# Weights start 64 bytes, no longer 192, past a multiple of 256 bytes in SBUF: attention over channels and a squared-ReLU FFN on one core

## The chip, the cores and the metric

The kernel runs on one core of a Trainium2 chip. The metric is the device time of one execution in microseconds (us); the time of a version is the median of its runs.

## What is computed

```
B, N, C = 4, 6080, 256;  d_ff = 2048
qn = q / (norm(q, axis=N) + 1e-6);  kn = k / (norm(k, axis=N) + 1e-6)
a  = softmax(kn^T @ qn / tau, last axis) (+ 1e-9)      # 256 x 256 for each of the 4 batches
x  = v @ a                                             # 24320 tokens x 256
h  = relu(x @ w_in)                                    # 256 -> 2048
out = (h * h) @ w_out                                  # 2048 -> 256
```

q, k, v and the output are float32; w_in and w_out arrive as float64, and the kernel makes a high and a low part of each.

## The kernel before

Attention and the first FFN product are folded into one: for each batch the kernel makes W = a @ w_in and then computes relu(v @ W). Tokens stand along the free axis and channels on the partitions. A number is held as a high and a low part (float32r), and each product is three products: high x high, high x low, low x high. Of the 12 token blocks of a batch ten have 512 tokens and the last two 480; after the first two blocks of the program each product of a 2x2 block form is made with seven block products, so that a matmul streams half a block, 256 or 240 columns.

In every matmul of TensorE one operand is fixed (the weights, 128 columns of 4 bytes, 512 bytes in each partition) and one moves (256 or 240 columns, up to 1,024 bytes in a partition). For each matmul the weights are loaded anew; the loading of the next matmul's weights runs while this one streams.

The work is written out as a repeating period (`PERIOD`, `period(k)`), a group of 42 matmuls of the first product and 42 (in six early groups 45) of the second each:

- `first_B`, `second_B` write ps_b, `first_H`, `second_H` ps_h, `copy_C`, `second_C`, `third_C`, `fourth_C` ps_c: six matmuls each, weights from the tiles wf (reloaded for each group from HBM by `load_forms`), moving operands v_hi and v_lo;
- `window_A1` to `window_A3` and `window_S` write ps_o: weights from W_out's own parts (wo_hi, wo_lo) or from sums of them (wS_hi, wS_lo, wS_odd_hi, wS_odd_lo), moving operands A_hi, A_lo, s_hi, s_lo;
- beside them stand the gram of the next batch's q and k (`products`, weights and moving operand both in qk_parts) and the forming of W (ps_w: weights eT_hi, eT_lo).

Where a tile begins in a partition follows from the order of the pools and the sizes ahead of it. In bytes, modulo 256, before the change:

| operands | tiles | start modulo 256 |
|---|---|---|
| fixed | wo_hi, wo_lo (pool const) | 192 |
| fixed | wf, w_hi, w_lo (wpool); wS, wS_odd, eT (wsums); the k half of qk_parts (the first tile of pool) | 192 |
| moving | v_hi, v_lo, A, s1, s2, g parts, the q half of qk_parts | 0 |

The two halves of qk_parts are `HALF` elements (4,096 bytes) apart and `GAP` elements more, which sets the second half, and all tiles of pool behind it, to 0. The seven blocks of v_hi and v_lo follow each other (`T1, B11, T3, B21, B22, T2, T4 = range(7)`). A block of 256 columns is 1,024 bytes, so that all seven begin at 0; a block of 240 columns is 960 bytes, so that blocks 0 to 6 begin at 0, 192, 128, 64, 0, 192, 128.

Of the kernel before, what the change touches and what calls it, by code (L numbers as in the profile page):

```python
# [10 lines left out]
F32 = mybir.dt.float32  # L11
# [21 lines left out]
def kernel(  # L33
# [26 lines left out]
    P = 128  # L60
# [38 lines left out]
    const = ctx.enter_context(tc.tile_pool(name="const", bufs=1))  # L99
# [24 lines left out]
    rinv_room = const.tile([P, NC], F32, name="rinv_room")  # L124

    HALF = NC * GRP
    GAP = 16

    def parts_room(name, dt):

        return pool.tile([P, 2 * HALF + GAP], dt, tag="qk_parts", name=name, bufs=1)

    scalar.activation(parts_room("first", F32)[:, 0:1], exp_bias, AF.Square)
    wo_hi = const.tile([P, NF, C], F32R, name="wo_hi")
    wo_lo = const.tile([P, NF, C], F32R, name="wo_lo")
    late = {}

    def two_parts(name, dt, shape):

        room = parts_room(name, dt)  # L140
        halves = room[:, 0:HALF], room[:, HALF + GAP :]
        return [half.rearrange("p (a b) -> p a b", a=shape[1]) if len(shape) > 2 else half for half in halves]

    def rounded_qk(name):
# [3 lines left out]
        for at in (0, J * C):  # L148
            of_k = room[:, at : at + J * C]
            both = bass.AP(of_k.tensor, of_k.offset, [of_k.ap[0], [HALF + GAP, 2], of_k.ap[1]])  # L150
            parts.append(both.rearrange("p a (j c) -> p a j c", j=J))
# [1435 lines left out]
```

## Time and profile before

| | |
|---|---|
| median of 3 runs | 2107.0 us (2104.4 to 2107.66) |
| the profiled execution | 2107.39 us, its span 2105.6 us, 1.8 us around it |
| TensorE (PE), share of the span | 2100.4 us, 100%, 17,158 matmul records |
| VectorE (DVE), ScalarE (ACT), GpSimd (POOL) | 90%, 89%, 17% |
| granted TensorE clock | 1.00 |
| DMA | 261 GB/s on average |

A busy PE is not a PE at its peak: the end of a matmul is modelled and lies behind the start of the next one. What a matmul costs on PE is read from one start to the next. 17,158 is more than the 17,011 matmuls of the program, since a float32 product stands as two records.

### The profile page before, as it was taken

Reading aid. Unit: us, or ns where it says so; the run is one execution under the profiler, and the core shown is the slowest. Engines: PE = TensorE matmul, PEld = TensorE weight load, DVE = VectorE, ACT = ScalarE, POOL = GpSimd, SP = SyncE. Lnnn points to the kernel's source line nnn. Section 1 sums busy time; section 2 is a strip of 40 time slices with the busy share of each in tenths; the row PEclk is TensorE's granted clock in tenths of the full one; section 3 lists DMA queues with packets and bytes.
Section 4 is the critical chain, followed back from the end, with each engine's and each line's share of the span. In section 5 each row is a group of like instructions: output and inputs, shape, how many; then the busy total and the mean of one; then the engine's idle time right before and its main releaser. Section 6 shows DMA issues by size and latency. Waiting matters only on the chain.

```text
span 2105.6 us, 43463 instructions
## 1 busy us (share of the span) xinstructions
PE 2100.4 (100%) x17158; PEld 2065.7 (98%) x17158; DVE 1905.2 (90%) x2195; ACT 1879.6 (89%) x2379; POOL 350.2 (17%) x430
## 2 busy tenths in 40 slices
PE   9999999999999999999999999999999999999999
PEld 8789999999999999999999999999999999999999
DVE  7898999989999999989998999998999888888887
ACT  5888999889999999889989999998988988988987
POOL 0000111111121111111122111211111121121112
PEclk9999999999999999999999999999999999999999
DMA  9777888789999888788999978878999787787775
GB/s 357 224 230 274 247 267 250 243 253 309 307 278 317 257 247 255 237 253 281 292 299 277 308 251 260 247 243 248 287 278 304 233 239 246 235 242 243 232 242 154
DMA packets 258012, 549.78 MB, mean 261 GB/s; under 512 B 26672, under 2 KB 113072, under 8 KB 257808
## 3 DMA queue, kind: packets, MB, share of 16 engines
q1 hardware_dynamic: 201456, 469.02, 65.0%
q0 software_dynamic: 56352, 77.98, 18.6%
q8 instruction: 135, 2.21, 0.4%
q14 instruction: 69, 0.57, 0.1%
HBM read 433.59 MB, written 58.72 MB: 234 GB/s over the span
## 4 chain that ended last, share of the span: by engine, by line
PE 99%; ACT 0%; DVE 0%; issue 0%; DVEq 0%; ACTq 0%
PE ps_o L29 45%; PE ps_c L29 18%; PE ps_h L29 14%; PE ps_b L29 12%; PE gram L29 7%; PE ps_w L29 2%; PE ps_end L29 0%; PE ps_first L29 0%; PE ps_n L29 0%; ACT x L29 0%; PE ps_t L29 0%; DVE x L29 0%; DVE w_lo L29 0%; ACT A_hi L29 0%; ACT ps_c L29 0%
## 5 line engine op out<-in xcount | busy, mean ns | idle before, releaser
L29 PE MATMUL ps_c<-v_hi,wf 128*128 128x256 f32 (+1 forms) x2208 | 477.1, 279 | 0.3 <-DVE x L29 0.2
L29 DVE TENSOR_TENSOR x<-x 128x1024 f32<-128x1024 f32 (+2 forms) x549 | 464.9, 847 | 11.1
L29 POOL DMA_DIRECT2D o<-o x225 | 232.6, 1188 | 1401.6 <-ACT o L29 903.4
L29 DVE TENSOR_TENSOR s_lo<-x,s_hi 128x1024 fp32r<-128x1024 f32 (+1 forms) x366 | 441.2, 1207 | 16.6 <-ACT s_hi L29 16.2
L29 ACT ACTIVATE x<-x 128x1536 f32<-128x1536 f32 (+4 forms) x384 | 405.2, 1055 | 42.5 <-DVE x L29 38.9
L29 ACT CAST s_hi<-x 128x1024 fp32r<-128x1024 f32 (+1 forms) x366 | 382.3, 1044 | 50.1 <-DVE x L29 49.1
L29 DVE TENSOR_TENSOR A_lo<-x,A_hi 128x1536 fp32r<-128x1536 f32 (+2 forms) x183 | 313.5, 1713 | 83.1 <-ACT A_hi L29 75.0
L29 PEld LDWEIGHTS ps_c<-v_hi,wf 128*128 128x128 f32 x2208 | 375.4, 188 | 1.1 <-DVE x L29 0.4
L29 PE MATMUL ps_b<-v_hi,wf 128*128 128x256 f32 (+1 forms) x1472 | 317.3, 278 | 0.0
L29 PE MATMUL ps_h<-v_hi,wf 128*128 128x256 f32 (+1 forms) x1472 | 317.3, 278 | 0.0
L29 PE MATMUL ps_c<-v_lo,wf 128*128 128x256 f32 (+1 forms) x1104 | 307.5, 279 | 0.0
L29 ACT CAST A_hi<-x 128x1536 fp32r<-128x1536 f32 (+2 forms) x183 | 264.1, 1443 | 0.0
L29 PEld LDWEIGHTS ps_h<-v_hi,wf 128*128 128x128 f32 x1472 | 250.4, 188 | 0.0
L29 PEld LDWEIGHTS ps_b<-v_hi,wf 128*128 128x128 f32 x1472 | 250.3, 188 | 0.1
L29 PEld LDWEIGHTS ps_c<-v_lo,wf 128*128 128x128 f32 x1104 | 207.5, 188 | 0.1
L29 PE MATMUL ps_h<-v_lo,wf 128*128 128x256 f32 (+1 forms) x736 | 204.9, 278 | 0.0
L29 PE MATMUL ps_b<-v_lo,wf 128*128 128x256 f32 (+1 forms) x736 | 204.8, 278 | 0.0
L29 PE MATMUL ps_o<-A_hi,wo_hi 128*128 128x256 f32 (+1 forms) x897 | 193.3, 279 | 0.0
L29 PE MATMUL ps_o<-A_lo,wo_hi 128*128 128x256 f32 (+1 forms) x897 | 193.0, 279 | 0.0
L29 PE MATMUL ps_o<-A_hi,wo_lo 128*128 128x256 f32 (+1 forms) x897 | 192.6, 279 | 0.0
L29 ACT COPY x<-ps_c 128x512 f32<-128x512 f32 (+1 forms) x184 | 107.2, 582 | 53.1 <-PE ps_c L29 42.7
L29 PE MATMUL ps_o<-s_hi,wS_hi 128*128 128x256 f32 (+1 forms) x549 | 153.0, 279 | 0.0
(172 smaller groups left out, 5197.6 us busy)
## 6 DMA issues: line engine op xcount, KB each, us to landing
wf<-wf_kept SPq DMA_DIRECT2D x368, 512.0 KB, 5.2
wf<-wf_kept SPq DMA_DIRECT2D x368, 384.0 KB, 4.8
o<-o POOLq DMA_DIRECT2D x114, 256.0 KB, 5.0
qk<-in_k SPq DMA_DIRECT2D x88, 256.0 KB, 5.3
qk<-in_q SPq DMA_DIRECT2D x88, 256.0 KB, 5.4
v<-in_vT SPq DMA_DIRECT2D x76, 256.0 KB, 4.8
out_T<-o POOLq DMA_DIRECT2D x152, 128.0 KB, 5.1
wf_kept<-wS SPq DMA_DIRECT2D x64, 256.0 KB, 6.5
```

The costliest lines, as they stand in the source:

```text
L29: return lambda *args, **kwargs: self.tc.keep_in_program_order(issue(*args, **kwargs))
```

## The change

No instruction, no wait and no queue changes, and on each engine the instructions stand in the same order as before; only addresses move. `GAP` grows from 16 to 48 elements (64 to 192 bytes), and a tile of 32 elements (128 bytes) that nothing uses is put behind wo_lo.

```
-    GAP = 16
+    GAP = 48
...
     wo_hi = const.tile([P, NF, C], F32R, name="wo_hi")
     wo_lo = const.tile([P, NF, C], F32R, name="wo_lo")
+    const.tile([P, 32], F32, name="between")
```

By the tiles' addresses in the two programs: wo_hi and wo_lo stay at 192. All tiles of wpool and wsums and the first half of qk_parts go from 192 to 64 (192 + 128 = 320 = 256 + 64). The second half of qk_parts and the tiles behind it stay at 0 (64 + 4,096 + 192). So the distance from the moving operand's start to the fixed one's, modulo 256, goes from 192 to 64 for 9,876 float32r matmuls of 256 columns and stays 192 for 3,702 of them. For 1,902 of 2,694 matmuls of 240 columns the weights go to 64 as well, and for 384 of 576 of 512 columns. In PE's order weights at 64 and at 192 then follow each other in 3,034 places, where before all these stood at 192. In 72 float32 matmuls of the first gram (weights and moving operand in the same tile of wpool) both go from 192 to 64.

## Rows read from the trace of the kernel before

**Rows 1.** The page: engines, clock by slices, the chain that ended last

```profile
PE 2100.4 (100%) x17158; PEld 2065.7 (98%) x17158; DVE 1905.2 (90%) x2195; ACT 1879.6 (89%) x2379; POOL 350.2 (17%) x430
...
PEclk9999999999999999999999999999999999999999
...
PE 99%; ACT 0%; DVE 0%; issue 0%; DVEq 0%; ACTq 0%
```

**Rows 2.** PE's waits: line, releaser, us in total, times, longest

```profile
PE ps_first L29 <- DVE single L29: 1.1, 1, 1.1
PE ps_c L29 <- DVE x L29: 0.2, 1, 0.2
```

**Rows 3.** Stretches: length, busy us (count) by engine, clock, DMA share, GB/s

```profile
602.47:875.24 272.77, 272.77 (x2318) 272.77 (x2317) 256.35 (x271) 256.23 (x315) 50.49 (x62) 1.00 0.85 260
...
545.46:585.87 40.41, 40.41 (x362) 40.41 (x360) 37.41 (x46) 36.77 (x49) 7.95 (x10) 1.00 1.00 314
...
155.00:2095.00 1940.00, 1939.74 (x16424) 1931.58 (x16423) 1769.37 (x2016) 1760.21 (x2234) 343.98 (x418) 1.00 0.85 262
```

**Rows 4.** PE's timeline at 408 us: start, length, instruction, count

```profile
407.89 0.40 PE L29 MATMUL ps_c<-v_hi,wf 128*128 128x256 f32 x2
...
408.83 0.28 PE L29 MATMUL ps_o<-A_lo,wS_hi 128*128 128x256 f32 x1
408.95 0.28 PE L29 MATMUL ps_o<-A_lo,wo_hi 128*128 128x256 f32 x1
```

**Rows 5.** PE's timeline at 418 us, the same work one period later

```profile
417.55 0.29 PE L29 MATMUL ps_c<-v_hi,wf 128*128 128x256 f32 x1
417.68 0.28 PE L29 MATMUL ps_c<-v_lo,wf 128*128 128x256 f32 x1
417.79 0.39 PE L29 MATMUL ps_c<-v_hi,wf 128*128 128x256 f32 x2
...
418.81 0.28 PE L29 MATMUL ps_o<-A_lo,wo_hi 128*128 128x256 f32 x1
```

**Rows 6.** Groups by shape: count, busy us, mean modelled ns, idle before

```profile
L29 PE MATMUL ps_c<-v_hi,wf 128*128 128x256 f32 x1824 | 396.4, 280 | 0.1
L29 PE MATMUL ps_h<-v_hi,wf 128*128 128x256 f32 x1216 | 264.0, 279 | 0.0
...
L29 PE MATMUL ps_c<-v_lo,wf 128*128 128x256 f32 x912 | 254.5, 279 | 0.0
...
L29 PE MATMUL ps_o<-s_hi,wS_lo 128*128 128x256 f32 x456 | 127.5, 280 | 0.0
...
L29 PE MATMUL gram<-qk_parts 128*128 128x256 f32 x792 | 104.5, 279 | 0.0
L29 PE MATMUL ps_o<-s_lo,wS_odd_hi 128*128 128x256 f32 x292 | 81.7, 280 | 0.0
...
L29 PE MATMUL ps_c<-v_hi,wf 128*128 128x240 f32 x384 | 80.7, 276 | 0.2 <-DVE x L29 0.2
L29 PE MATMUL ps_b<-v_hi,wf 128*128 128x240 f32 x256 | 53.4, 274 | 0.0
L29 PE MATMUL ps_h<-v_hi,wf 128*128 128x240 f32 x256 | 53.3, 273 | 0.0
...
L29 PE MATMUL ps_o<-A_hi,wS_hi 128*128 128x256 f32 x152 | 42.7, 281 | 0.0
```

**Rows 7.** The chain in blocks of 240 columns: start, us, work, count

```profile
546.30 0.67 PE ps_c L29 x6
...
548.32 0.67 PE ps_b L29 x6
548.99 0.67 PE ps_h L29 x6
```

**Rows 8.** The first gram: duration min/median/max ns, first and last start

```profile
L29 PE MATMUL gram<-qk x208: 377/379/763, 4.2 to 69.7; 128*128 128x256 f32 x104
L29 PE MATMUL gram<-qk_heads x32: 379/379/379, 48.1 to 55.3; 128*128 128x256 f32 x32
```

## The prediction

> **What bounds the kernel now.** I read the page first. PE is busy all through the span, the chain that ended last is 99% PE, and the granted clock is 1.00 in every slice, which is the upper of its two levels, 2.4 GHz [rows 1]. The view of waits then says whether PE is held up by others: in all it waits 1.1 us at the start and 0.2 us once later [rows 2]. From 155 to 2095 us VectorE works 1,769 us of 1,940 and ScalarE 1,760 [rows 3], so both have over 170 us of slack there. The time is therefore the number of matmuls by what one costs, from start to start.
>
> What one costs is read from stretches. From 602.47 to 875.24 us 2,318 matmuls of 256 columns are counted, of which two began before (a modelled end lies behind the next start), so that 272.77 us / 2,316 = 117.78 ns [rows 3]. 256 columns at 2.4 GHz are 106.67 ns: 11.1 ns of each are something else. The timeline shows that this rest is not fixed. At 408 us nine matmuls (from the second ps_c pair on) take 408.95 - 407.89 = 1.06 us, 117.8 ns each [rows 4]. The same nine steps of the next period, with the same tiles, take 418.81 - 417.79 = 1.02 us, 113.3 ns each [rows 5]. What differs is what came just before: one matmul there took 417.68 - 417.55 = 0.13 us. So a matmul of the same addresses has two paces, and a jolt of some 10 ns moves PE from one to the other; each then lasts, the slow one for 2,316 matmuls on end. The reader is to see in this that the 4.5 ns hang on how the loading of weights and the streaming of columns stand in time to each other. Addresses may enter there, since both read the same partitions.
>
> **The change part by part.** It removes and adds no instruction, wait or transfer. What it moves is where weights begin. In the groups by shape the float32r matmuls of 256 columns whose weights go from 192 to 64 are ps_c 1,824 + 912, ps_h and ps_b 1,216 + 608 each, the gram 792, three groups like wS_lo of 456, three like wS_odd of 292 and three like A_hi,wS_hi of 152 [rows 6]: 6,384 + 792 + 1,368 + 876 + 456 = 9,876. They cost 9,876 x 117.78 ns = 1,163 us of the span.
>
> *The price of distance 64 against 192* stands nowhere in blocks of 256 columns, since all moving operands begin at 0 and all weights at 192. Blocks of 240 columns are nearest. There the blocks begin at 0, 192, 128, 64, 0, 192, 128. ps_h (blocks T1 and B22, both at 0) has distance 192, as nearly all has now. ps_c is for two thirds (T3 and T4, at 128) at distance 64, as the change makes it; its other third (T2) and half of ps_b have distance 0. Six matmuls of ps_c, ps_b and ps_h take 0.67 us each in the chain [rows 7]. Read to 0.01 us that is a difference of at most 1.7 ns for one matmul. The modelled means are 276, 274 and 273 ns [rows 6]; they order the distances, 64 as the dearest, but are no start-to-start times. The bounds by these rows: 0 to +1.7 ns, 0 to +17 us for 9,876.
>
> *The price of the pace.* In the blocks of 240 columns, where the distance changes from block to block, no pace holds: 40.41 us / 360 = 112.25 ns [rows 3], 12.25 over their 100 ns of columns. The two paces of 256 columns are 11.1 and 6.67 ns over. So the other bound is a gain: if all 9,876 fell to 113.33 ns, 9,876 x 4.45 = 44 us, and if the 1,902 matmuls of 240 columns came as near to their columns (106.7 ns), 1,902 x 5.6 = 11 us more, together 55 us. I take the middle of this for the likeliest, half of the 9,876 at the fast pace: 4,938 x 4.45 = 22 us. The reason for a gain at all: the slow pace is now a lock in which each matmul finds the same positions; with weights half a turn of 256 bytes further, and 3,034 changes between 64 and 192 in PE's order, the place where loading meets streaming moves by 128 bytes and the long lock has to be found anew, while 113.33 ns is a pace that this kernel has shown itself to hold.
>
> *The rest costs nothing.* The 3,702 matmuls of 256 columns with W_out's own parts keep their distance; they stand between the others and may take over either pace, which the range has to bear. The first gram's float32 records take 377 to 379 ns with both operands at 192 (wpool) and at 0 (the other chunks, qk_heads) alike [rows 8], so moving both from 192 to 64 is taken as 0. VectorE, ScalarE and DMA write to other addresses in as many instructions; should some become slower, the 170 us of slack cover it. Were PE faster by all 55 us, over 110 us of it would be left, so neither becomes the bound on average.
>
> The sum: 2107.4 us of the profiled execution (0.4 over the median of the runs) - 22 = **2086 us**, rounded up.
>
> **A rule against it.** The Trainium skill ("SBUF — State Buffer", section "Who interferes with whom") gives PE two read ports, one for the moving operand and one for the weights, independent of each other. By it addresses would not matter and the sum would be 2107. Its page "TensorE: Matmul & The Clock Gate", section "Back-to-back issue gap", puts a warm matmul at N / 2.4 + 2.5 ns, an estimate of 109.2 ns for 256 columns, and lets the weight load have a say in a stream of both. The rows give 113.3 and 117.8 ns [rows 3 to 5], so the trace does not agree with a fixed gap; it does not show which address matters.
>
> **The rivals.**
> - *No change.* The two paces hang on the order in time alone, and the slow one is what PE falls into whatever the address. For it: six matmuls of ps_c, ps_b and ps_h cost the same 0.67 us at all distances [rows 7]. Against it: the modelled means of the same groups differ by 3 ns [rows 6]. Time: 2107 us.
> - *Slower.* The 3,034 changes between weights at 64 and at 192 leave no pace that holds, as in blocks of 240 columns. A matmul then costs its columns and 12.25 ns: 106.67 + 12.25 = 118.92 ns, 1.14 more than now. Over 9,876 that is 11 us, 2118 us; over all 13,578 of 256 columns 15 us, 2123 us. For it: blocks of 240 columns are the only place of this kernel where distances change, and there the rest over the columns is the largest. Against it: 240 columns may be too short to cover the loading of the next weights, which would put some of the 12.25 ns down to the loading and not to a meeting of the two. It decides as soon as the mean of the 256-column matmuls is over 118.1 ns (+4.2 us).
> - *All of it.* Every matmul with weights at 64 takes the fast pace: 2107 - 44 = 2063 us, with the 240-column ones 2052 us. For it: the pace exists. Against it: of the 2,316 matmuls from 602 to 875 us hardly one has it, or their mean would not be 117.78 ns [rows 3].
>
> **How the numbers follow.** A measurement of this kernel tells a change from none at about 0.2%, 4.2 us. A gain of some kind 0.46 (the half of it most likely, all of it 0.08), no change 0.20, slower 0.34. The range goes from 2056 us, where all 9,876 are fast and some of the 240-column ones, to 2124 us, where distance 64 costs its full 1.7 ns (2107 + 17). Outside it I leave 0.05 below and 0.08 above. The likeliest case alone would lie between 2070 and 2100 us.
>
> **What would show it.** Right: stretches of 256 columns with a mean between 113.3 and 117.8 ns, long runs of ps_b, ps_h and ps_c at 0.68 us for six, no longer 0.71, and unchanged 117.8 ns where only W_out's parts are the weights. Wrong: 117.8 ns as before in the long stretches (no change), or 118 to 120 ns with steps that vary from matmul to matmul (slower). PE's waits on VectorE growing from 0.2 us to several us would say that the gain is there and is taken by another engine. The reading is wrong as a whole if the two paces turn up in other places with the same addresses, so that chance and not the layout decides.

## The result, and the profile after

| | before | after |
|---|---|---|
| median | 2107.19 us (2104.4 to 2107.66, 4 runs) | 2069.51 us (2067.91 to 2070.7, 4 runs) |
| profiled execution, span | 2107.39 us, 2105.6 us | 2067.91 us, 2066.1 us |

The ratio is 0.9823 (95% interval 0.9806 to 0.984): 37.7 us faster, where 21 were predicted; the time lies in the range, and 0.5 us under the 2070 to 2100 us that were called the likeliest.

The page after, engines and the chain that ended last:

```profile
PE 2059.4 (100%) x17158; PEld 2017.0 (98%) x17158; DVE 1894.9 (92%) x2195; ACT 1869.8 (90%) x2379; POOL 350.5 (17%) x430
...
PE 94%; DVE 3%; ACT 2%; issue 0%; DMA 0%; DVEq 0%; ACTq 0%
```

PE is still busy all through, with as many records as before [rows 1], and the granted clock is 1.00 in every slice here too. But 5% of the chain now goes over VectorE and ScalarE, where it was 99% PE.

Stretches of the changed kernel (columns as in [rows 3]):

```profile
635.87:837.96 202.09, 202.09 (x1785) 202.09 (x1784) 198.29 (x208) 195.08 (x243) 38.20 (x47) 1.00 0.90 275
155.00:2060.00 1905.00, 1903.07 (x16464) 1887.66 (x16463) 1763.20 (x2024) 1752.10 (x2236) 344.46 (x418) 1.00 0.87 266
```

With two matmuls that began before, 202.09 us / 1,783 = 113.34 ns: the fast pace, held for 1,783 matmuls where before the slow one, 117.78 ns, was held for 2,316 [rows 3]. The second row is the one to compare with 155:2095 of [rows 3]: VectorE's and ScalarE's work stays the same to within 10 us, while the stretch for it is 35 us shorter.

PE's waits (columns as in [rows 2]):

```profile
PE ps_first L29 <- DVE single L29: 1.1, 1, 1.1
PE ps_c L29 <- DVE x L29: 0.9, 4, 0.3
PE ps_c L29 <- ACT x L29: 0.3, 1, 0.3
PE ps_o L29 <- DVE s_lo L29: 0.2, 1, 0.2
```

This view counts a wait only from the modelled end of the matmul before, some 0.16 us after the next could have begun, so short waits do not show in it. For all figures of this kind below I took the steps from one matmul's start to the next out of the trace. A step that is over 19 ns longer than its columns at 2.4 GHz is put down as a wait, with what it has over its columns and 7 ns; "without waits" leaves such steps out. That gives:

| from one start to the next | before | after |
|---|---|---|
| 256 columns, mean without waits | 117.75 ns | 113.81 ns |
| of these at 115 ns or less | 0.8% | 90.7% |
| 240 columns, mean without waits | 112.11 ns | 112.14 ns |
| waits, sum | 4.4 us | 18.2 us |

Some 13,400 matmuls x 3.94 ns are -53 us, the waits +14 us: -39 us, against 37.7 measured (39.5 between the two profiled spans).

What the waits look like stands in the chain of the changed kernel at 1626 us (start, us, work, count):

```profile
1625.35 0.68 PE ps_o L29 x6
1626.03 0.80 PE ps_c L29 x6
1626.84 1.41 PE ps_o L29 x12
1628.25 0.70 PE ps_b L29 x6
1628.95 0.68 PE ps_h L29 x6
1629.63 1.36 PE ps_o L29 x12
```

Six matmuls at the fast pace are 0.68 us and twelve 1.36. fourth_C's six ps_c take 0.80. The twelve behind them take 1.41, 117.5 ns each: the slow pace stands behind the wait. It ends within the next six (0.70), and 0.68 and 1.36 are back. Most of the waits stand at this place: by steps, 12.8 us at the first or the second matmul of a ps_c group, where the kernel before has 0.8.

The next such place, on the timeline (start, length, instruction):

```profile
1633.82 1.22 DVE L29 TENSOR_TENSOR x<-x 128x1024 f32<-128x1024 f32 x1
...
1634.96 0.68 DVE L29 CUSTOM_DVE_ANT_0 x<-x,ps_c 128x512 f32<-128x512 f32 x1
...
1635.70 0.38 PE L29 MATMUL ps_c<-v_hi,wf 128*128 128x256 f32 x1
...
1635.92 0.28 PE L29 MATMUL ps_c<-v_lo,wf 128*128 128x256 f32 x1
```

add_C (the second row) reads ps_c and ends at 1635.64; fourth_C, which writes ps_c again, starts at 1635.70 and its second matmul comes 0.22 us later, not 0.113. add_C started late because two_sums (the first row, 1.22 us) stood ahead of it on VectorE until about 1635.0; what taking it away does is seen in after_less_dve.

### The profile page after: what moved, and what is told of

It reads as the page before. It is cut to its first block, busy times and chain, and to the rows that moved or that the text cites. A ratio compares the mean times of both kernels' runs of the same rounds, so it can differ in the third digit from the quotient of the medians.

```text
span 2066.1 us, 43463 instructions
## 1 busy us (share of the span) xinstructions
PE 2059.4 (100%) x17158; PEld 2017.0 (98%) x17158; DVE 1894.9 (92%) x2195; ACT 1869.8 (90%) x2379; POOL 350.5 (17%) x430
## 4 chain that ended last, share of the span: by engine, by line
PE 94%; DVE 3%; ACT 2%; issue 0%; DMA 0%; DVEq 0%; ACTq 0%
PE ps_o L29 42%; PE ps_c L29 18%; PE ps_h L29 14%; PE ps_b L29 11%; PE gram L29 7%; PE ps_w L29 2%; DVE x L29 1%; ACT x L29 1%; DVE s_lo L29 1%; DVE A_lo L29 0%; ACT A_hi L29 0%; DMA wf<-wf_kept 0%; PE ps_end L29 0%; DVE wo_sums L29 0%; DVE acc L29 0%
## 5 line engine op out<-in xcount | busy, mean ns | idle before, releaser
L29 PE MATMUL ps_b<-v_hi,wf 128*128 128x256 f32 (+1 forms) x1472 | 310.3, 276 | 0.0
L29 PE MATMUL ps_h<-v_hi,wf 128*128 128x256 f32 (+1 forms) x1472 | 310.1, 276 | 0.0
L29 PE MATMUL ps_o<-s_lo,wS_hi 128*128 128x256 f32 (+1 forms) x549 | 151.6, 276 | 0.2 <-DVE s_lo L29 0.2
```

Source lines behind the costliest of these rows:

```text
L29: return lambda *args, **kwargs: self.tc.keep_in_program_order(issue(*args, **kwargs))
```

## The experiments

The first eight place the operands in other ways; none changes an instruction or the order. The last four ask where the waits come from. "Distance" is the start of the fixed operand less that of the moving one, modulo 256 bytes; "fast" is the share of the 256-column steps at 115 ns or less in the profiled execution. The kernel before took 2105.7 to 2107.2 us (medians) beside them. For gap_only and all_at_64 the profiled execution was the slowest of the four, so their shares are those of a slow execution and not of the median.

| kernel | distances of 256-column matmuls | time, us | ratio, 95% | mean step, fast |
|---|---|---|---|---|
| gap_only | 64 | 2077.38 (2073.55 to 2086.84) | 0.9871 [0.9845, 0.9896] | 115.9 ns, 42.5% |
| all_at_64 | 64 | 2079.85 (2074.33 to 2086.89) | 0.9878 [0.9852, 0.9904] | 115.68 ns, 48% |
| pad_only | 192; W_out's parts 64 (moving ones at 128) | 2070.0 (2068.33 to 2071.32) | 0.9829 [0.9814, 0.9843] | 114.08 ns, 84% |
| w_out_at_64 | 192; W_out's parts 64 | 2068.12 (2067.63 to 2068.68) | 0.982 [0.9803, 0.9836] | 114.16 ns, 82.5% |
| ws_moved | 192; wS 64 | 2069.06 (2067.7 to 2070.93) | 0.9826 [0.9811, 0.9841] | 114.02 ns, 85.7% |
| w_out_at_128 | 192; W_out's parts 128 | 2110.2 (2109.67 to 2111.13) | 1.0021 [1.0012, 1.003] | 117.94 ns, 6% |
| all_at_0 | 0 | 2137.09 (2136.97 to 2137.34) | 1.0149 [1.0132, 1.0166] | 119.94 ns, 0.2% |
| all_at_128 | 128 | 2120.56 (2120.16 to 2120.68) | 1.007 [1.0054, 1.0085] | 118.74 ns, 18.8%, single steps |

**gap_only** and **all_at_64**: all matmuls at distance 64, so that no two distances follow each other. The first has only the change's `GAP`, which leaves W_out's parts at 192 and puts moving operands at 128; the second has them at 64 and 0.

```
-    GAP = 16
+    GAP = 48
```

> Only GAP 48, no tile behind W_out: all weights stay at 192, the moving operands behind qk_parts go to 128, so every matmul of 256 columns has distance 64. Theory distance (the start of the weights against the start of the moving operand, modulo 256, sets the pace): 256-column matmuls at 113.3 ns in the long stretches, W_out's too, 2064 to 2074 us. Rival alternation (the changes between two distances in PE's order break the slow pace): there are none here, 117.8 ns, 2107 us. Rival absolute (weights that begin at 64 are faster to load than those at 192): no weights at 64, 117.8 ns, 2107 us.

```
-    GAP = 16
+    GAP = 48
...
+    const.tile([P, 32], F32, name="ahead")
     wo_hi = const.tile([P, NF, C], F32R, name="wo_hi")
```

> The tile of 128 bytes stands ahead of wo_hi, GAP 48: all weights, W_out's too, at 64, moving operands at 0; distance 64 for all. Theory distance: 113.3 ns, 2064 to 2074 us, as the version with GAP alone. Rival alternation: no alternation, 117.8 ns, 2107 us. Rival absolute: 2066 to 2070 us.

The two agree within their spread, so of the starts only the distance was seen to count, and "absolute" falls. Both are faster than before and slower than the change, so neither the time of "distance" (2064 to 2074 us) nor that of "alternation" (2107 us) is met. They vary by 13 us from run to run, where the change varies by 3. Two stretches of one execution of gap_only say why:

```profile
641.42:872.62 231.20, 231.20 (x1964) 231.20 (x1965) 220.87 (x233) 215.72 (x267) 39.54 (x49) 1.00 0.84 263
1154.13:1356.21 202.08, 202.08 (x1784) 202.08 (x1785) 198.35 (x208) 194.75 (x243) 38.37 (x47) 1.00 0.89 276
```

By their starts these are 1,963 steps of 117.78 ns and 1,783 of 113.33, the same work at the same addresses. With one distance a pace lasts until something else comes in between. Taking six steps on end at one pace as a pace, this execution has 46 changes of it: 31 without a wait at blocks of 240 columns, 15 at a wait, and none within a stretch of 256 columns without either. Distance 64 thus has the same two paces as 192 and costs nothing by itself. The two paces stand in one execution, and the time differs from run to run; that each run deals them out differently is read from this, only one execution having a trace.

**pad_only** and **w_out_at_64**: two distances in turn, but 9,876 matmuls at 192 and W_out's 3,702 at 64, the change the other way round.

```
     wo_lo = const.tile([P, NF, C], F32R, name="wo_lo")
+    const.tile([P, 32], F32, name="between")
```

> Only the tile of 128 bytes behind W_out, GAP 16: weights outside W_out at 64, W_out's at 192, moving operands at 128. Distance: 192 as before for 9,876 matmuls of 256 columns, 64 for W_out's 3,702. Theory distance: the 9,876 keep 117.8 ns; 2091 us if W_out's own matmuls take 113.3 ns each by themselves, 2107 us if they follow the pace of those around them. Rival alternation: distances alternate as in the change, 2070 us. Rival absolute: weights at 64 in the same 9,876 as in the change, 2070 us.

```
+    const.tile([P, 32], F32, name="ahead")
     wo_hi = const.tile([P, NF, C], F32R, name="wo_hi")
     wo_lo = const.tile([P, NF, C], F32R, name="wo_lo")
+    const.tile([P, 32], F32, name="between")
```

> The mirror of the change: 128 bytes ahead of wo_hi and 128 behind wo_lo, GAP 16: W_out's parts at 64, all other weights at 192, moving operands at 0. Distances as in the version with the tile alone, at other absolute places. Theory distance: the same time as that one, 2091 to 2107 us. Rival alternation: 2070 us. Rival absolute: only W_out's 3,702 faster, 2091 us.

Both are as fast as the change, with most weights at the old distance. "Distance" falls. What brings the fast pace nearly everywhere is the taking turns, "alternation"; the fast pace can be held without it too, as gap_only shows, but not reliably. pad_only is also the change without its `GAP` line: the one tile of 128 bytes gives the whole gain, and the `GAP` line alone (gap_only) some three quarters of it, with the spread. The timeline of w_out_at_64 shows the slow pace end at such a place (wS and wf at 192, wo at 64):

```profile
193.43 0.40 PE L29 MATMUL ps_c<-v_hi,wf 128*128 128x256 f32 x2
...
194.14 0.28 PE L29 MATMUL ps_o<-A_lo,wS_hi 128*128 128x256 f32 x1
194.25 0.28 PE L29 MATMUL ps_o<-A_hi,wo_hi 128*128 128x256 f32 x1
194.37 0.28 PE L29 MATMUL ps_o<-A_hi,wo_lo 128*128 128x256 f32 x1
194.48 0.28 PE L29 MATMUL ps_o<-A_lo,wo_hi 128*128 128x256 f32 x1
194.60 0.28 PE L29 MATMUL ps_b<-v_hi,wf 128*128 128x256 f32 x1
...
195.50 0.39 PE L29 MATMUL ps_h<-v_hi,wf 128*128 128x256 f32 x2
```

From 193.43 to 194.14 are six steps, 118 ns each; then come three matmuls with weights at 64, and from 194.48 to 195.50 nine steps of 113.3 ns, with weights at 192 again. No wait stands between. With six steps on end as a pace, slow turned to fast in this way, at a change of distance or a few steps behind one and without a wait, 44 times here, 44 in pad_only, 32 in ws_moved and 39 in the change. Not every change does it: in the same order, the slow pace passed 368, 322, 384 and 135 such changes without ending there. The fast pace passed 1,845, 1,890, 3,015 and 2,072 and ended near one without a wait never, once, three times (and twice more with no change near) and never. Fast ends at a wait instead, 47 times here, or at blocks of another column count, five times.

**ws_moved**: the kernel before with wS alone at 64, 1,824 matmuls, as a smaller share of the work with more changes (4,368).

```
         def __init__(self):
+            wsums.tile([P, 32], F32, tag="ahead", name="ahead", bufs=1)
             self.room = [
...
+            wsums.tile([P, 32], F32, tag="behind", name="behind", bufs=1)
             self.raws, self.gens, self.parts = {}, {}, {}
```

> Before, but wS_hi and wS_lo alone begin at 64 (128 bytes ahead of and behind them in their pool): 1,824 of 13,578 matmuls of 256 columns at distance 64, all others at 192, moving operands at 0; weights change between 64 and 192 in 4,368 places of PE's order. Theory change of distance (with one distance the pace, once taken, lasts until the next wait; a change of distance ends the slow pace and leaves the fast one): the fast pace nearly everywhere, 2066 to 2075 us, though nine tenths of the weights stay where they were. Rival share (each matmul at distance 64 is faster by itself): 1,824 x 4.4 ns = 8 us, 2098 us.

Moving 1,824 matmuls gave all of the gain, as "change of distance" had it. It does not go by the share of matmuls that are moved.

**w_out_at_128**: as many changes as w_out_at_64, between 192 and 128.

```
+    const.tile([P, 48], F32, name="ahead")
     wo_hi = const.tile([P, NF, C], F32R, name="wo_hi")
     wo_lo = const.tile([P, NF, C], F32R, name="wo_lo")
+    const.tile([P, 16], F32, name="between")
```

> Before, but W_out's parts at 128 (192 bytes ahead of wo_hi, 64 behind wo_lo): distances 128 and 192 alternate in 3,041 places, 64 does not occur. Theory change of distance: any two distances do, 2066 to 2075 us. Rival 64 (the pair must hold a distance of 64): 2107 us.

Slower than before by 0.2%. So not just any two distances do, and that part of "change of distance" falls.

**all_at_0** and **all_at_128**: one distance, 0 or 128.

```
-    GAP = 16
+    GAP = 64
...
+    const.tile([P, 16], F32, name="ahead")
     wo_hi = const.tile([P, NF, C], F32R, name="wo_hi")
```

> All weights at 0 (64 bytes ahead of wo_hi, GAP 64), moving operands at 0: one distance, 0. Theory change of distance: no changes, so the pace is found at waits and kept; the runs differ among themselves by several us, as with all weights at 64 (13 us between them), or lie at 2107 us, and none is at 2068 us. Rival conflict (the same start is the worst, since loading and streaming then ask for the same place): over 2115 us.

```
-    GAP = 16
+    GAP = 32
...
+    const.tile([P, 48], F32, name="ahead")
     wo_hi = const.tile([P, NF, C], F32R, name="wo_hi")
```

> All weights at 128 (192 bytes ahead of wo_hi, GAP 32), moving operands at 0: one distance, 128. Theory change of distance: as with all at 0. Rival conflict: 128 is the furthest from the same start, 2068 us.

A stretch of all_at_0:

```profile
608.82:886.72 277.90, 277.90 (x2318) 277.90 (x2317) 257.07 (x271) 257.29 (x315) 50.56 (x62) 1.00 0.83 255
```

And the same work in all_at_128:

```profile
605.64:880.48 274.84, 274.84 (x2318) 274.84 (x2318) 256.58 (x271) 256.66 (x315) 50.48 (x62) 1.00 0.84 259
```

277.90 / 2,316 = 119.99 ns and 274.84 / 2,316 = 118.67 ns. At 0 nearly every step (97%) is 120 ns; at 128 the steps go round by 117, 122, 120, 119 and 115 ns or stay at 120. Neither has a run of 113.33 ns anywhere. So "change of distance", which gave 0 and 128 the same two paces, is wrong here, and "conflict" is right for 0 and wrong for 128, the furthest from the same start, where it had 2068 us. It goes with this that w_out_at_128 wins nothing, since 128 has no fast pace that a change could lead to; that this is the reason is not shown, for most of its matmuls stand at 192, which has one.

**after_less_dve** and **before_less_dve**: two_sums left out of the changed kernel and of the one before.

```
         (0, third_C),
-        (1, two_sums),
```

> The changed kernel with two_sums left out of the period: two of the four blocks of x are then not the differences that W_out's products need, so the output is another one; every other instruction stays. That takes 1.22 us per period from VectorE, just ahead of add_C, for which PE is seen waiting at fourth_C. Theory given back: of the gain in pace PE now loses about 14 us in short waits for x, and each also leaves the slow pace behind until the next change of weights. Without two_sums the waits go: 2069 - 14 = 2055, and up to 5 us less for the matmuls that then stay fast: 2050 to 2056 us, with over 95% of the 256-column matmuls at the fast pace. Rival: the longer steps are no waits for VectorE but jolts of the pace itself: 2067 to 2070 us, and the steps of 0.2 us at ps_c remain.

> The kernel before with two_sums left out (the same part of the computation as in the run beside it). Theory given back: before the change VectorE held PE up hardly at all, so there is little to win: 2102 to 2107 us, and 117.8 ns for each matmul of 256 columns. Rival, by which less work on VectorE makes PE's matmuls or its weight loads faster by itself (all read and write the same partitions): as much is gained here as in the run beside it, 2090 to 2095 us.

after_less_dve: 2054.89 us (2053.72 to 2055.5), ratio 0.9756 [0.9743, 0.9769], 14.6 us under the change. Its page and one stretch:

```profile
PE 2046.0 (100%) x17158; PEld 2009.8 (98%) x17158; DVE 1695.5 (83%) x2012; ACT 1862.4 (91%) x2379; POOL 349.8 (17%) x430
```

```profile
1597.88:1963.80 365.92, 365.92 (x3231) 365.92 (x3230) 286.56 (x318) 333.49 (x423) 74.02 (x90) 1.00 0.82 249
```

By their starts 3,228 steps on end, 113.36 ns each. The waits fall from 18.2 to 6.0 us (those at ps_c from 12.8 to 1.2) and the mean step from 113.81 to 113.68 ns: 12.2 + 1.7 of the 14.6 us. The time is in the forecast's 2050 to 2056 us; the share at the fast pace is 93%, not over 95%.

before_less_dve: 2101.39 us (2096.4 to 2107.43, 12 runs), ratio 0.998 [0.9969, 0.999], 4.4 us under the kernel before beside it. It is not waits that it wins: they are 4.2 us (4.4 in the kernel before). In its profiled execution, the fastest (2096.4), the mean step is 116.95 ns: 13,500 x 0.8 = 11 us, all that its span has less than that of before. The chain there:

```profile
470.24 0.68 PE ps_c L29 x6
470.92 1.36 PE ps_o L29 x12
472.27 0.68 PE ps_b L29 x6
```

So with all weights at 192 the fast pace is held too, here from 427 to 503 us and in two later stretches of some 116 us. Each time it begins behind the four ps_t matmuls of the softmax between two batches and ends at the blocks of 240 columns. That it is chance which pace PE comes out with there is not shown; the 12 runs differ by 11 us, as much as these three stretches are worth. VectorE's load by itself made no matmul faster, for the other stretches stay at 117.8 ns, the one of [rows 3] too:

```profile
602.47:875.24 272.77, 272.77 (x2319) 272.77 (x2318) 229.14 (x251) 254.87 (x315) 50.24 (x62) 1.00 0.85 259
```

**add_c_sooner**: add_C ahead of two_sums.

```
         (0, third_C),
+        (0, add_C),
         (1, two_sums),
...
-        (0, add_C),
```

> The changed kernel with add_C ahead of two_sums in the period, nothing else. add_C then begins when third_C's last matmul ends, about 0.6 us sooner than now, and fourth_C no longer waits for it; two_sums comes about 0.7 us later, and third_sum, last_sum, hi_S behind it. Theory given back: 2069 less most of the 14 us of waits, 2055 to 2062 us, if VectorE's time is what it has too little of only at this place. Rival: VectorE now idles up to 0.5 us per period until third_C has ended, with 0.7 us per period free at best; the waits turn up at the next place (ps_o waiting for s_hi and s_lo) and the time is 2069 us or more.

2156.97 us (2152.36 to 2160.77), ratio 1.0237 [1.0222, 1.0251]. Its waits:

```profile
ACT s_hi L29 <- DVE x L29: 238.7, 169, 2.9
...
DVE x L29 <- PE ps_c L29: 74.6, 91, 1.8
...
PEld ps_o L29 <- DVE s_lo L29: 40.5, 71, 2.8
PEld ps_c L29 <- ACT ps_c L29: 32.2, 70, 0.8
```

The rival, but at a price that neither theory had. VectorE now waits for third_C's ps_c, 74.6 us (12.3 in the change); two_sums and all behind it come later, and s_hi, s_lo and copy_C with them. PE's steps hold 104.7 us of waits, 86.5 more than the change; the time is 87.5 us longer. The matmuls stay at 114.0 ns.

**v_sums_gpsimd**: the three sums of v on GpSimd; one of the three lines:

```
...
-            vector.tensor_sub(raw[:, T2, :], raw[:, B22, :], raw[:, T1, :])
+            pool_engine.tensor_sub(raw[:, T2, :], raw[:, B22, :], raw[:, T1, :])
...
```

> The changed kernel with the three sums of each block of v (sum_in_v) on GpSimd and no longer on VectorE, at the same places. VectorE loses three instructions of 0.42 to 0.69 us per block of v, some 70 us in all, in the periods in which it also makes v_lo; GpSimd works only 17% of the span. Theory given back: PE's waits for add_C stand in the periods in which VectorE has most to do; without the sums of v a part of the 14 us comes back: 2058 to 2066 us. Rival: the sums now stand in GpSimd's queue behind its own issues of output transfers, which wait for ScalarE, and are slower there; v_lo comes later, PE waits at ps_b and ps_h, and VectorE's own instructions get longer beside GpSimd's: 2070 to 2120 us.

2097.97 us (2095.32 to 2100.33), ratio 0.996 [0.9948, 0.9973]: 28.5 us over the change, though VectorE has 138 instructions less. Groups by shape in this kernel:

```profile
L29 POOL TENSOR_TENSOR v<-v 128x256 f32<-128x256 f32 x76 | 98.5, 1295 | 6.0
...
L29 DVE TENSOR_TENSOR x<-x 128x1024 f32<-128x1024 f32 x146 | 196.3, 1344 | 5.1
L29 DVE CUSTOM_DVE_ANT_0 x<-x,ps_c 128x512 f32<-128x512 f32 x152 | 103.3, 679 | 8.6 <-PE ps_c L29 6.0 <-ACT x L29 2.6
```

and in the changed kernel:

```profile
L29 DVE TENSOR_TENSOR x<-x 128x1024 f32<-128x1024 f32 x146 | 178.9, 1225 | 5.1
L29 DVE CUSTOM_DVE_ANT_0 x<-x,ps_c 128x512 f32<-128x512 f32 x152 | 103.5, 681 | 8.5 <-PE ps_c L29 5.6 <-ACT x L29 2.8
```

A sum of v of 256 columns takes GpSimd 1,295 ns, and some of VectorE's own instructions grow meanwhile: two_sums, with both inputs in SBUF, from 1,225 to 1,344 ns in the mean, while add_C, with one of its two in PSUM (ps_c), stays at 680. VectorE's busy time is 1,894.3 us as before the move (1,894.9): the work taken off it came back whole, as longer instructions. PE's waits are 44.3 us, 26 more, most of them at ps_c and not, as the rival had it, at ps_b and ps_h. The Trainium skill ("SBUF — State Buffer", section "Who interferes with whom") says that a VectorE instruction with two SBUF inputs contends with a GpSimd instruction that reads SBUF. This trace agrees (1,225 to 1,344 ns).

## Why the prediction was right, and where its numbers were off

- **The reading of the bound** held. The time is the number of matmuls by their step, and two paces of the same work, 117.78 and 113.33 ns, were what the addresses moved. Of PE's waits the prediction missed a second one of 0.2 us (at ps_h), which changes nothing.
- **"The price of the pace" was mis-sized.** It took half of 9,876 matmuls as fast, 22 us, and the half was the middle of a range that no row of the trace pointed to. It was 91% of all 13,400, 53 us. The range was wide enough (2056 to 2124 us) to hold this and the opposite sign; a gain had a chance of 0.46, so that the sign was in part luck. The 3,702 with W_out's parts, of which "The rest costs nothing" said only that they "may take over either pace", became as fast as the others (114.05 ns against 113.73), and the forecast of "unchanged 117.8 ns where only W_out's parts are the weights" was wrong. The 11 us held possible for blocks of 240 columns came to nothing (112.11 and 112.14 ns).
- **The reason given for it held in one half.** That the changes between 64 and 192 end "the long lock" is what the steps show: the slow pace ends at some of them (39 times in the change, while 135 others did not end it), the fast one at none of 2,072. The other half, that the weights' new distance counts, fell with pad_only, w_out_at_64 and ws_moved.
- **"The price of distance 64 against 192"** is nothing, the lower bound: 113.33 and 117.78 ns occur at both (gap_only; before and before_less_dve). The modelled means, which had 64 as the dearest, misled.
- **"Neither becomes the bound on average"** was true and beside the point. VectorE kept 140 us free, but at one place of some periods add_C comes too late. The prediction had named the sign ("PE's waits on VectorE growing from 0.2 us to several us"); by steps it is 14 us more, and after_less_dve gives 12 of them back.
- **The rivals.** "Slower" had the 3,034 changes of distance as its mechanism, and just these carry the gain. "All of it" came nearest in size: 2063 us for 9,876 fast matmuls; the change has more of them and the waits on top. "No change" falls, yet its reading, that order in time alone sets the pace, is what one distance shows (gap_only).
- **The sign of being wrong as a whole**, the two paces "in other places with the same addresses, so that chance and not the layout decides", came up where there is one distance: gap_only and all_at_64 vary by 13 us, before_less_dve by 11. With two distances in turn it did not: the change varies by 3.
- **The rule against it.** The distance sets steps of 120.0 ns (0), 118.7 (128), and 117.8 or 113.3 (64, 192). The Trainium skill ("SBUF — State Buffer", section "Who interferes with whom") has PE's port for the moving operand independent of that for the weights; the traces do not agree that the two operands' starts are without effect on each other. Its page "TensorE: Matmul & The Clock Gate", section "Back-to-back issue gap", gives N / 2.4 + 2.5 ns (an estimate of 109.2 ns for 256 columns) for a single matmul by itself and has the spacing in a stream set by weight load and matmul together. The steps of 113.3 to 120.0 ns lie over the estimate; what the weight load adds was not measured by itself here. The prediction compared that formula with a stream, for which the page does not mean it.

What stays open is why distances 0 and 128 have no pace of 113.33 ns, and what in PE makes some changes between 64 and 192 end the slow pace and nearly all spare the fast one. The runs show that it is so, not how. Only multiples of 64 bytes were tried. That a wait can bring the slow pace is seen from what stands before it in the trace (41 times in the change; five times a wait stood before the fast pace), and after_less_dve has fewer of both; no wait was added by itself.

No version tried that computes the reference beats the change by more than the measurement tells: w_out_at_64 and ws_moved lie within 1.5 us of it. All of the gain is to be had with one unused tile of 128 bytes (pad_only), and a further 14 us lie in what PE waits for VectorE, mostly add_C, which two ways of moving work did not reach.

## What to carry to other kernels

Where PE is the bound and each matmul loads its weights anew, measure the step from start to start in stretches without waits and look whether the same work shows two steps; if it does, the starts of fixed and moving operands modulo 256 bytes are worth a try, and so is giving a few of the weights another distance than the rest (here 64 against 192; 128 against 192 won nothing). Repeat runs too: a layout with one distance was faster here in the median and 13 us apart from run to run. What an engine that got faster then waits for can be too short for the view of waits (here 2.5 us in it, 18.2 by steps): compare steps, not idle time. Slack of an engine on average says little; what counts is whether the one instruction that PE needs starts in time, and moving that one or its neighbours can cost more than the wait.

## What the hardware showed that was not expected

- A matmul's step in float32r depends on the distance of the two operands' starts: 1.5% of this kernel's time between 0 and 192, and 3.3% between 0 and the best mix (2137.09 against 2068.12).
- Two steps of the same work at the same addresses, each held for over 1,700 matmuls (1,963 at 117.78 ns, 1,783 at 113.33 ns in one execution), and with them a time that varies by 13 us with nothing changed.
- A single unused tile of 128 bytes took the kernel from 2105.8 to 2070.0 us (pad_only).
- 138 instructions moved from VectorE to GpSimd left VectorE's busy time where it was (1,894.9 and 1,894.3 us).
